# Load order of batch 0, opening tiles of the first product, and the place of one scale and two stores, in a linear-attention plus ELU-MLP kernel

## The chip, the cores and the metric

The kernel runs on one core of a Trainium2 chip. The metric is the device time of one execution in microseconds (us); the kernel before has a median of 288.38 us over 5 runs (287.56 to 288.8).

## The reference

```python
# attention, per batch b (8) and head h (8), 576 rows of 64
kv  = einsum('bhsd,bhse->bhde', k, v)
out = einsum('bhsd,bhde->bhse', q, kv)
x   = out / sqrt(mean(out*out, -1) + 1e-6) * g_norm      # then heads side by side: 4608 x 512
# MLP
h = x @ w_in                                             # 4608 x 2048
g = where(h > 0, h, exp(min(h, 0)) - 1)
y = g @ w_out                                            # 4608 x 512, float32
```

## The kernel before, in words

**Tiling.** The 4608 rows are worked in nine groups T = 0 to 8 of 512 rows. A group needs `xT[T]`, the normalised attention output turned so that the 512 features lie on partitions (four chunks of 128). The first product (`h_ps`, lines 382 and, at the start, 570) gives eight tiles i = 0 to 7 of 2 x 128 columns of `w_in`; each is an accumulation over the four chunks in a pair of PSUM banks, tagged A, B, or "mx" (one bank of the pool m, one of x). `elu` turns a tile into `gT` with an exponential on ScalarE (L350) and two VectorE instructions (L362, L366; the second reads PSUM and so sets when the pair is free again), or, where `relu` is given, with a Relu on ScalarE (L355) that frees the pair early. The second product (`o_ps`, L403) multiplies `gT` by `w_out`; ScalarE copies a result out (L419) and `store` sends halves of a group to memory through SyncE's queue (L461 to L464).

**The order is written by hand.** Each engine executes its instructions in the order in which the Python code emits them; a wait holds everything behind it on that engine or queue.

**The start (lines 468 to 652).** Batch 0 comes in chunks of heads: q chunks 0 and 2, k chunk 0 and v chunk 0 through SyncE's queue, the rest through GpSimd's load queue (`chunk_load`, L90; `load_w_in`, L116), which casts to bf16 on the way. Group 0 is normalised chunk by chunk: `chunk_kv` (L156), its copy `chunk_kv_out`, `chunk_y` (L189), `chunk_square` (L552), `mean_mm` (L199), an inverse root on ScalarE and `chunk_scale` (L212 on VectorE). `early(tiles, c)` issues the first product's matmuls (L570) of chunk c as soon as that chunk is there, in the order 0, 2, 1, 3, so that tiles are opened on chunk 0 and closed on chunk 3. `idle(n)` issues matmuls on zeros.

**The rest (lines 661 to 802).** In group T's window the attention part of group T+1 runs between the matmuls: `kv`, and for each half h of the rows `se` (product and squares), `sum` (L283), `inv` (L291, L292), `mul` (L299 on VectorE, then two DMA transposes on SyncE's queue, L306, which bring the scaled half into `xT`) and `gain` (L312 on VectorE, the multiplication by g_norm). `ahead` turns q of batch T+2 by two DMA transposes on SyncE's queue (L331); a copy on GpSimd (`gate`, L339) waits for them, and only then are the loads of the next batch issued. The dictionaries `early` and `late` say after which tile i each piece is emitted: `early` between tile i's matmuls and its `rest` (L362, L366), with the second-product half in `second[i]` emitted after the early pieces; `late` after the `rest`.

For T = 2 two tiles are *opened*: both get their matmuls over the first 256 rows (the half whose `gain0` comes first) before the second 256 rows are needed.

Of the kernel before, what the change touches and what calls it, by code (L numbers as in the profile page):

```python
# [16 lines left out]
def kernel(  # L17
# [16 lines left out]
    B, H, S, D = q.shape  # L34
# [5 lines left out]
    KC = DM // P  # L40
# [51 lines left out]
    def fetch_ahead(b):  # L92
        raw[b] = stage.tile([P, 4, RK, D], FP32, name="st_q", tag="q")
        load(raw[b], "q", b)
        for name in "kv":
            fetch(name, b)

    def cast_q(b):

        bf["q", b] = qkvp.tile([P, 2, RK, 2, D], BF16, name="q_bf", tag="q")  # L100
        for js in (slice(0, 3), slice(3, 6), slice(6, 9)):
            for u in range(2):
                nc.gpsimd.tensor_copy(  # L103
                    out=bf["q", b][:, u, js],
                    in_=raw[b][:, u::2, js, :].rearrange("p l j d -> p j l d"),
                )

    def copy_on(eng, out_, in_):
        if eng is nc.scalar:
            nc.scalar.copy(out_, in_)  # L110
        else:
            eng.tensor_copy(out=out_, in_=in_)  # L112

    def load_w_in(fs, cs=slice(0, KC)):
        cols = slice(fs.start * P, fs.stop * P)
        nc.gpsimd.dma_start(  # L116
            out=w_in_sb[:, cs, cols], in_=moe_w_in.rearrange("(c p) f -> p c f", p=P)[:, cs, cols]
        )
# [10 lines left out]
    def single(tag, name):  # L129
        pool = ps_x if tag == "x" else ps_m2  # L130
        return pool.tile([P, 512], FP32, name=name, tag=tag)

    def pair(tag, name):
        if tag in ("x", "m", "mx"):
            return [single(t, name) for t in (tag + tag)[:2]]
        return ps_m1.tile([P, 2, 512], FP32, name=name, tag=tag)
# [61 lines left out]
    def mean_mm(sq, ps):  # L198
        nc.tensor.matmul(ps, lhsT=ones, rhs=sq, start=True, stop=True)  # L199
# [4 lines left out]
    def r_tile():  # L204
        return outp.tile([P, 2, G], FP32, name="rT", tag="o")
# [5 lines left out]
    def scale_t(T, ps, r, cs, cols=slice(0, 512)):  # L211
        nc.vector.scalar_tensor_tensor(  # L212
            out=xT[T][:, cs, cols], in0=ps, scalar=g_col, in1=r, op0=ALU.mult, op1=ALU.mult
        )
# [113 lines left out]
    def turn_q(b):  # L328
        qt = qT_tile(b)
        for s in range(2):  # L330
            nc.sync.dma_start_transpose(  # L331
                out=qt[:, s].rearrange("p u j r -> p (u j) r"),
                in_=bf["q", b][s * 64 : s * 64 + 64].rearrange("p u j l d -> p (u j l d)"),
            )

    def after_turn(b):

        gate = const.tile([1, 2, 16], BF16, name="gate")
        nc.gpsimd.tensor_copy(out=gate, in_=qT[b][0:1, :, 1, RK - 1, 0:16])  # L339
# [35 lines left out]
    def g_tile(T):  # L375
        gT[T] = mlpg.tile([P, FC, G], BF16, name="gT", tag="gT")

    def mm1_part(T, i, ps, cs, cols=slice(0, 512), last=True):
        for a in range(2):
            f = 2 * i + a  # L380
            for n, c in enumerate(cs):
                nc.tensor.matmul(  # L382
                    (ps[a] if isinstance(ps, list) else ps[:, a, :])[:, cols],
                    lhsT=w_in_sb[:, c, f * P : f * P + P],
                    rhs=xT[T][:, c, cols],
                    start=(c == 0),
                    stop=(last and n == len(cs) - 1),
                )
# [62 lines left out]
    def mm2_half(T, i):  # L451
        mm2(T, i // 2, 8 * (i % 2), 8 * (i % 2) + 8)
# [31 lines left out]
    def chunk_load(name, cs):  # L484
        ms = slice(cs[0], cs[-1] + 1, 2)
        load(bf[name, 0][:, ms], name, 0, ms)
# [3 lines left out]
    chunk_load("q", (1, 3))  # L490
    chunk_load("k", (1,))
    chunk_load("v", (1,))
    load_w_in(slice(0, 6), slice(0, 1))
    chunk_load("k", (3,))
    chunk_load("v", (3,))
    for c in (2, 1, 3):
        load_w_in(slice(0, 6), slice(c, c + 1))
    for lo, hi in ((6, 8), (8, 12), (12, 16)):
        load_w_in(slice(lo, hi))
# [24 lines left out]
    def idle(n, ps):  # L524
        for _ in range(n):
            nc.tensor.matmul(ps, lhsT=zeros[:, 0:P], rhs=zeros, start=True, stop=True)
# [10 lines left out]
    def chunk_kv(kv_ps, c):  # L537
        kv_mm(0, [kv_ps[:, s, :] for s in range(2)], c % 2, (c // 2,))

    def chunk_kv_out(kv_ps, c, eng):  # L540
        rows, cols = slice(c // 2 * 64, c // 2 * 64 + 64), slice(c % 2 * 64, c % 2 * 64 + 64)
        copy_on(eng, kv_sb[rows, 0, c % 2], kv_ps[rows, :, cols])
# [3 lines left out]
    def chunk_y(c, ps):  # L546
        y_ps[c] = ps
        y_mm(0, c % 2, {c // 2: ps}, (c // 2,))

    def chunk_square(c):  # L550
        sq0[c] = attp.tile([P, G], BF16, name="sq", tag="sq")
        nc.scalar.activation(sq0[c], y_ps[c], AF.Square)  # L552

    def chunk_scale(c, r, cols=slice(0, 512)):
        scale_t(0, y_ps[c][:, cols], r[:, cols], c, cols)

    def chunk_norm(c, mean):

        r = r_tile()[:, 0, :]
        nc.scalar.activation(r, mean, AF.Ln, bias=eps_col)  # L560
        for n in range(2):
            cols = slice(n * 256, n * 256 + 256)
            nc.scalar.activation(r[:, cols], r[:, cols], AF.Exp, scale=-0.5)
            chunk_scale(c, r, cols)

    def early(tiles, c):

        for i, a in tiles:
            h = h_ps[i]
            nc.tensor.matmul(  # L570
                h[a] if isinstance(h, list) else h[:, a, :],
                lhsT=w_in_sb[:, c, (2 * i + a) * P : (2 * i + a) * P + P],
                rhs=xT[0][:, c, :],
                start=(c == 0),
                stop=(c == KC - 1),
            )
# [16 lines left out]
    mean = pair("A", "mean")[:, 0, :]  # L593
# [11 lines left out]
    r = r_tile()  # L605
    inv_t(r[:, 0, :], mean)
    mean = single("m", "mean")
# [5 lines left out]
    h_ps = [pair("A", "h_ps")]  # L613
# [4 lines left out]
    chunk_y(1, single("m", "y_ps"))  # L618
    chunk_square(1)
    chunk_scale(0, r[:, 0, :])  # L620
    chunk_scale(2, r[:, 1, :])
    early([(0, 0), (0, 1)], 0)
    mean = single("m", "mean")
    chunk_kv(kv_ps, 3)
    chunk_kv_out(kv_ps, 3, V)
    mean_mm(sq0[1], mean)
    r = r_tile()
    nc.scalar.activation(r[:, 0, :], mean, AF.Ln, bias=eps_col)
    y3 = single("x", "y_ps")
    h_ps += [None, [single("x", "h_ps"), None]]  # L630
    early([(2, 0)], 0)
    chunk_y(3, y3)
    chunk_square(3)
    for n in range(2):
        cols = slice(n * 256, n * 256 + 256)
        nc.scalar.activation(r[:, 0, cols], r[:, 0, cols], AF.Exp, scale=-0.5)
        chunk_scale(1, r[:, 0, :], cols)
    h_ps[1] = pair("B", "h_ps")
    early([(1, 0), (1, 1)], 0)
    early([(0, 0), (0, 1)], 2)  # L640
    mean_mm(sq0[3], mean)
    chunk_norm(3, mean)
    early([(2, 0), (1, 0), (1, 1)], 2)
    early([(0, 0), (0, 1), (1, 0), (1, 1), (2, 0)], 1)
    h_ps[2][1] = single("m", "h_ps")
    for c in (0, 2, 1):
        early([(2, 1)], c)
    early([(0, 0), (0, 1), (1, 0), (1, 1), (2, 0), (2, 1)], 3)
    for i in range(3):
        elu(0, i, h_ps[i], i == 1)()  # L650
    for i, tag in zip(range(3, 8), ("mx", "A", "B", "mx", "mx")):
# [116 lines left out]
    for T in range(2, NT):  # L768
        at, early, late = {}, {}, {}
        if T + 1 < NT:  # L770
            at = attention(T + 1)
            if T + 2 < B:
                cast_q(T + 2)

                def ahead(b=T + 2):
                    turn_q(b)
                    if b + 1 < B:
                        after_turn(b)
                        fetch_ahead(b + 1)
                at["ahead"] = ahead  # L780
            else:
                at["ahead"] = lambda: None
            early = {2: ("sum0", "inv0"), 4: ("sum1", "inv1"), 5: ("gain0",), 7: ("gain1",)}
            late = {0: ("kv",), 1: ("se0",), 2: ("mul0",), 3: ("se1",), 4: ("mul1", "ahead")}
        if T == 2:
            early = {2: ("sum0", "inv0"), 5: ("sum1", "inv1"), 6: ("gain0",), 7: ("gain1",)}
            late = {0: ("kv",), 1: ("se0",), 2: ("mul0",), 4: ("se1",), 5: ("mul1", "ahead")}
        halves = {1: 5, 3: 6, 5: 7} if T == 2 else {0: 1, 1: 3, 2: 4, 3: 5, 4: 6, 5: 7}
        second = {i: (lambda n=n: mm2_half(T - 1, n)) for i, n in halves.items()}
        if T > 2:  # L790
            window(T, at, early, late, second)
        else:
            g_tile(T)
            opened = [pair(tag, "h_ps") for tag in "BA"]
            for i in range(2):
                mm1_part(T, i, opened[i], range(KC), slice(0, 256))
            window(T, at, early, late, second, (3, 5), opened)
        mm2_half(T, 0)
        mm2_half(T, 2)
# [33 lines left out]
```

## Time and profile before

| quantity | value |
|---|---|
| median of 5 runs | 288.38 us (287.56 to 288.8) |
| the profiled execution's own time | 288.72 us |
| its span, first to last instruction | 286.2 us |
| TensorE matmul (PE) busy | 277.9 us, 97% |
| VectorE (DVE), ScalarE (ACT), GpSimd (POOL) busy | 57%, 49%, 17% |
| granted TensorE clock | 1.00 throughout |

Times in the views are microseconds from the span's start. PE and PEld are TensorE's matmuls and weight loads; SPq is SyncE's queue. A chain or timeline row gives start, duration, engine, line, output and input, and a count; brackets give the idle time before and what ended it. A row of the waits gives who waited for whom, the total, how often, and the longest. Ends of matmuls are modelled: one 128x512 matmul is shown as 0.38 us, but eight of them take 1.73 us in the chain, so one slot is 0.216 us.

### The profile page before, as it was taken

The numbers are of one execution on the slowest core, as the hardware profiler recorded it, in microseconds if no ns is written. First come the engines' busy times: TensorE is split into PE (matmuls) and PEld (weight loads), VectorE is DVE, ScalarE is ACT, GpSimd is POOL, SyncE is SP. The second block draws the span as 40 slices with busy tenths as digits, with TensorE's granted clock in tenths as the row PEclk, the third lists the DMA queues.
The fourth block names the chain that finished last, engine by engine and source line by source line (L and its number), as shares of the span: only waits on it lengthen the run. The fifth ranks groups of instructions, "written<-read, shape, count | busy, mean of one in ns | idle before, by whom it ended". The sixth has DMA issues, their size and how long they took to land.

```text
span 286.2 us, 5167 instructions
## 1 busy us (share of the span) xinstructions
PE 277.9 (97%) x2131; PEld 129.8 (45%) x2131; DVE 164.5 (57%) x222; ACT 141.4 (49%) x209; POOL 47.9 (17%) x89
## 2 busy tenths in 40 slices
PE   8899999999999899999999999999999999999994
PEld 3444444444644344444444444444444444444443
DVE  2439632966487547853776278727763776344600
ACT  4578359594468155425553455335543554333311
POOL 8643303203114033004200330000000000000000
PEclk9999999999999999999999999999999999999999
DMA  7999999999999769679936993632150235030222
GB/s 213 181 205 206 206 261 235 176 274 165 169 256 126 148 159 251 88 127 265 199 31 117 257 217 46 110 85 73 39 110 0 73 39 110 0 76 0 73 73 74
DMA packets 50571, 39.46 MB, mean 138 GB/s; under 512 B 30964, under 2 KB 44020, under 8 KB 50548
## 3 DMA queue, kind: packets, MB, share of 16 engines
q0 software_dynamic: 15008, 21.30, 37.2%
q1 hardware_dynamic: 35136, 17.31, 31.6%
q10 hardware_dynamic: 404, 0.53, 0.5%
q8 instruction: 16, 0.26, 0.4%
q14 instruction: 7, 0.06, 0.1%
HBM read 36.70 MB, written 9.44 MB: 161 GB/s over the span
## 4 chain that ended last, share of the span: by engine, by line
PE 87%; DMA 6%; DVE 3%; ACT 1%; issue 1%; POOL 0%; DVEq 0%; SPq 0%; POOLq 0%
PE o_ps L403 41%; PE h_ps L382 40%; DMA w_in_sb<-in_moe_w_in_dram 3%; DMA v_bf<-in_v_dram 2%; PE at L250 2%; PE at L156 1%; DVE gT L366 1%; PE o_ps L440 1%; DMA xT<-xs 1%; PE h_ps L570 1%; ACT elu_e L350 1%; DVE elu_e L362 1%; PE qt_ps L174 0%; DVE xs L299 0%; PE mean L199 0%
## 5 line engine op out<-in xcount | busy, mean ns | idle before, releaser
L382 PE MATMUL h_ps<-xT,w_in_sb 128*128 128x512 bf16 (+1 forms) x568 | 128.1, 373 | 2.1 <-DVE xT L312 1.2
L403 PE MATMUL o_ps<-w_out_sb,gT 128*128 128x512 bf16 x560 | 129.7, 379 | 0.0
L350 ACT ACTIVATE elu_e<-h_ps 128x1024 bf16<-128x1024 f32 (+1 forms) x79 | 74.0, 952 | 91.7 <-PE h_ps L382 89.8
L403 PEld LDWEIGHTS <-gT 128*128 128x128 bf16 x560 | 54.4, 98 | 65.6 <-issue 0.9
L382 PEld LDWEIGHTS <-w_in_sb 128*128 128x128 bf16 x568 | 53.9, 98 | 63.3 <-DVE xT L312 1.7
L366 DVE TENSOR_TENSOR gT<-elu_e,h_ps 128x1024 bf16<-128x1024 bf16 (+1 forms) x67 | 77.2, 1157 | 6.9 <-PE h_ps L382 0.5
L362 DVE TENSOR_SCALAR elu_e<-elu_e 128x1024 bf16<-128x1024 bf16 x72 | 31.5, 438 | 64.8 <-ACT elu_e L350 64.7
L419 ACT COPY o_sb<-o_ps 128x512 f32<-128x512 f32 x32 | 18.3, 587 | 21.1 <-PE o_ps L403 21.1
L103 POOL CAST q_bf<-st_q 128x384 bf16<-128x384 f32 x36 | 16.8, 510 | 36.7 <-DMA st_q<-in_q_dram 30.3
L283 DVE TENSOR_REDUCE ss<-sq 128x16 f32<-128x1024 bf16 x14 | 17.1, 1220 | 6.8 <-ACT sq L277 6.8
L299 DVE TENSOR_TENSOR xs<-at,ss 128x1024 bf16<-128x1024 f32 x14 | 17.0, 1218 | 1.2 <-ACT ss L292 1.2
L277 ACT ACTIVATE sq<-at 128x1024 bf16<-128x1024 f32 x14 | 14.4, 1028 | 0.0
L339 POOL COPY gate<-qT 1x32 bf16<-1x32 bf16 x5 | 1.0, 200 | 66.2 <-DMA qT<-q_bf 66.2
L212 DVE SCALAR_TENSOR_TENSOR xT<-y_ps,g_col,rT 128x512 bf16<-128x512 f32 (+1 forms) x10 | 6.1, 639 | 10.0 <-ACT rT L209 7.9
L312 DVE TENSOR_SCALAR xT<-xT,g_col 128x1024 bf16<-128x1024 bf16 x14 | 6.7, 480 | 5.1 <-DMA xT<-xs 5.0
L355 ACT ACTIVATE elu_h<-h_ps 128x1024 bf16<-128x1024 f32 (+1 forms) x12 | 9.3, 817 | 0.0
L156 PEld LDWEIGHTS <-k_bf 64*64 64x64 bf16 x576 | 6.3, 107 | 5.2 <-issue 4.7
L90 POOL DMA_DIRECT2D v_bf<-in_v_dram x11 | 7.6, 694 | 4.2 <-DMA w_in_sb<-in_moe_w_in_dram 2.1
L90 POOL DMA_DIRECT2D k_bf<-in_k_dram x11 | 7.7, 700 | 2.6 <-DMA w_in_sb<-in_moe_w_in_dram 1.8
L250 PEld LDWEIGHTS <-qT 64*128 64x128 bf16 (+1 forms) x248 | 4.3, 97 | 6.1 <-issue 5.9
L112 DVE COPY o_sb<-o_ps 128x256 f32<-128x256 f32 x1 | 0.4, 424 | 11.1 <-PE o_ps L440 11.1
L366 DVE TENSOR_TENSOR gT<-elu_e,elu_h 128x1024 bf16<-128x1024 bf16 x9 | 6.2, 692 | 0.9
(57 smaller groups left out, 102.2 us busy)
## 6 DMA issues: line engine op xcount, KB each, us to landing
st_q<-in_q_dram POOLq DMA_DIRECT2D x6, 1152.0 KB, 7.5
out_dram<-o_sb SPq DMA_DIRECT2D x24, 256.0 KB, 4.1
k_bf<-in_k_dram POOLq DMA_DIRECT2D x6, 576.0 KB, 9.9
v_bf<-in_v_dram POOLq DMA_DIRECT2D x6, 576.0 KB, 12.7
out_dram<-o_sb SPq DMA_DIRECT2D x19, 128.0 KB, 2.4
w_out_sb<-in_moe_w_out_dram POOLq DMA_DIRECT2D x4, 512.0 KB, 14.9
w_in_sb<-in_moe_w_in_dram POOLq DMA_DIRECT2D x2, 512.0 KB, 11.0
q_bf<-in_q_dram POOLq DMA_DIRECT2D x3, 288.0 KB, 13.4
```

The source lines that it names most:

```text
L90: eng.dma_start(out=dst.rearrange("p m j d -> p m (j d)"), in_=in_[:, ms, :])
L103: nc.gpsimd.tensor_copy(out=bf["q", b][:, u, js], in_=raw[b][:, u::2, js, :].rearrange("p l j d -> p j l d"),)
L250: nc.tensor.matmul(se_ps[lo:hi, l, (4 * i + m) * 64 : (4 * i + m) * 64 + 64], lhsT=qT[b][l * 64 : l * 64 + 64, s, u, j : j + n, :], rhs=kv ...
L277: nc.scalar.activation(sq, st["se", h], AF.Square)
L283: nc.vector.reduce_sum(out=ss, in_=st.pop(("sq", h)).rearrange("p l (m e) -> p (l m) e", e=D), axis=AX.X,)
L299: nc.vector.tensor_tensor(out=st["xs"][:, 2 * h : 2 * h + 2, :].rearrange("p i (l m e) -> p l i m e", l=2, e=D), in0=se_ps.rearrange("p l ...
L350: nc.scalar.activation(e[:, lo:hi, :], h, AF.Exp)
L362: nc.vector.tensor_scalar(out=e, in0=e, scalar1=1.0, scalar2=1.0, op0=ALU.min, op1=ALU.subtract)
L366: nc.vector.tensor_tensor(out=gT[T][:, 2 * i + lo : 2 * i + hi, :], in0=e[:, lo:hi, :], in1=h, op=ALU.add if relu else ALU.max,)
L382: nc.tensor.matmul((ps[a] if isinstance(ps, list) else ps[:, a, :])[:, cols], lhsT=w_in_sb[:, c, f * P : f * P + P], rhs=xT[T][:, c, cols] ...
L403: nc.tensor.matmul(o_ps[T, j], lhsT=gT[T][:, f, j * P : j * P + P], rhs=w_out_sb[:, f, :], start=(f == 0), stop=(f == FC - 1),)
L419: nc.scalar.copy(o_sb[T, half][:, j % 2, :], o_ps[T, j])
```

## The change

Three parts.

1. On the load queue, the first chunk of `w_in` is loaded after k and v chunk 3 instead of before them.
2. In the start, `early` on chunk 0 no longer stands ahead of `chunk_kv(3)` and `chunk_y(3)`: one idle matmul stands there, all five tile halves (0,0), (0,1), (1,0), (1,1), (2,0) are opened together behind `chunk_y(3)`, `chunk_scale(2)` moves behind `chunk_kv_out(3)` on VectorE, and the last matmuls are put so that tile 0 closes one matmul earlier.
3. In T = 2's window, `mul1` (the second scale of group 3, with its two transposes) moves from behind tile 5's `rest` and second-product half to ahead of both; and only tile 0 (pair B) is opened on half its rows, tile 1 gets whole 512-row matmuls at its turn.

```diff
-    load_w_in(slice(0, 6), slice(0, 1))
     chunk_load("k", (3,))
     chunk_load("v", (3,))
-    for c in (2, 1, 3):
+    for c in (0, 2, 1, 3):
         load_w_in(slice(0, 6), slice(c, c + 1))
...
     chunk_scale(0, r[:, 0, :])
-    chunk_scale(2, r[:, 1, :])
-    early([(0, 0), (0, 1)], 0)
-    mean = single("m", "mean")
+    idle(1, h_ps[0][:, 0, :])
     chunk_kv(kv_ps, 3)
     chunk_kv_out(kv_ps, 3, V)
+    chunk_scale(2, r[:, 1, :])
+    mean = single("m", "mean")
     mean_mm(sq0[1], mean)
...
-    early([(2, 0)], 0)
     chunk_y(3, y3)
     chunk_square(3)
+    h_ps[1] = pair("B", "h_ps")
+    early([(0, 0), (0, 1), (1, 0), (1, 1), (2, 0)], 0)
     for n in range(2):
...
-    h_ps[1] = pair("B", "h_ps")
-    early([(1, 0), (1, 1)], 0)
     early([(0, 0), (0, 1)], 2)
     mean_mm(sq0[3], mean)
     chunk_norm(3, mean)
-    early([(2, 0), (1, 0), (1, 1)], 2)
+    early([(1, 0), (1, 1), (2, 0)], 2)
     early([(0, 0), (0, 1), (1, 0), (1, 1), (2, 0)], 1)
     h_ps[2][1] = single("m", "h_ps")
-    for c in (0, 2, 1):
-        early([(2, 1)], c)
-    early([(0, 0), (0, 1), (1, 0), (1, 1), (2, 0), (2, 1)], 3)
+    early([(2, 1)], 0)
+    early([(2, 1)], 2)
+    early([(0, 0), (0, 1)], 3)
+    early([(2, 1)], 1)
+    early([(1, 0), (1, 1), (2, 0), (2, 1)], 3)
...
         if T == 2:
-            early = {2: ("sum0", "inv0"), 5: ("sum1", "inv1"), 6: ("gain0",), 7: ("gain1",)}
-            late = {0: ("kv",), 1: ("se0",), 2: ("mul0",), 4: ("se1",), 5: ("mul1", "ahead")}
+            early = {2: ("sum0", "inv0"), 5: ("sum1", "inv1", "mul1"), 6: ("gain0",), 7: ("gain1",)}
+            late = {0: ("kv",), 1: ("se0",), 2: ("mul0",), 4: ("se1",), 5: ("ahead",)}
...
-            opened = [pair(tag, "h_ps") for tag in "BA"]
-            for i in range(2):
-                mm1_part(T, i, opened[i], range(KC), slice(0, 256))
+            opened = [pair("B", "h_ps")]
+            mm1_part(T, 0, opened[0], range(KC), slice(0, 256))
             window(T, at, early, late, second, (3, 5), opened)
```

## The prediction

> **What bounds the kernel now.** I read the page first: PE is busy for 277.9 of 286.2 us, so a change pays only where PE stands still. Then the chain of waits in order of time, to see where it leaves PE:
>
> ```profile
> 7.72 9.24 DMA w_in_sb<-in_moe_w_in_dram
> ...
> 17.00 2.35 PE h_ps L570 x10
> ...
> 22.23 7.07 PE h_ps L382 x32
> ...
> 63.00 8.75 PE o_ps L403 x40
> ...
> 72.39 2.78 PE h_ps L382 x24
> ...
> 91.38 1.22 DVE xs L299
> ...
> 94.98 2.50 DMA xT<-xs
> ...
> 97.51 0.50 DVE xT L312
> ...
> 98.05 1.90 PE h_ps L382 x8
> ```
>
> After 98.05 it is PE without a break until 282.38. The waits of PE after the first ten us:
>
> ```profile
> PE h_ps L382 <- DVE xT L312: 1.2, 1, 1.2
> PE h_ps L382 <- ACT o_sb L419: 0.7, 1, 0.7
> ...
> PE h_ps L382 <- DVE gT L366: 0.3, 1, 0.3
> ```
>
> These are three places: the opening of T=3 (98.05), of T=2 (72.39) and tile 4 of T=0 (22.23). Two timelines say what is behind the first two: VectorE's between 61 and 76 us, and SyncE's queue between 60 and 104 us:
>
> ```profile
> 71.80 0.48 DVE L312 TENSOR_SCALAR xT<-xT,g_col 128x1024 bf16<-128x1024 bf16 x1 [1.88 <-DMA xT<-xs]
> 72.73 0.49 DVE L312 TENSOR_SCALAR xT<-xT,g_col 128x1024 bf16<-128x1024 bf16 x1 [0.44 <-DMA xT<-xs]
> ```
>
> ```profile
> 62.13 8.06 SPq L306 DMA_TRANSPOSE xT<-xs  x4
> ...
> 91.42 1.29 SPq L461 DMA_DIRECT2D out_dram<-o_sb  x2
> 92.80 3.44 SPq L306 DMA_TRANSPOSE xT<-xs  x2
> 96.33 3.59 SPq L331 DMA_TRANSPOSE qT<-q_bf  x2
> ```
>
> T=2 opens on a landing: VectorE is idle until the first half of xT is there, gain0 ends at 72.28 and PE starts at 72.39. The 0.7 is booked on the copy L419 only because that ends last (72.35); the first opened tile does not use its pair. T=3 opens on the second half of xT, whose transposes stand behind two stores.
>
> **Part 3, mul1 ahead of the stores.** sum1 (L283) ends at 90.33; ScalarE's two steps end at 90.70 + 0.22 = 90.92. The scale L299 starts at 91.38 only because tile 5's L362 and L366 (90.25, 90.77) stand ahead of it. Moved ahead of them it runs from 90.96 to 92.18. The transposes no longer follow the two stores: first issue at 92.24 instead of 92.80, taking about 1.25 us (the pair at 84.93 takes 2.60) instead of 2.13, so the second goes at 93.5 instead of 94.98. With its own 2.50 us to land: 96.0, gain1 to 96.5, PE at 96.55. PE is through with the work before at 93.26 + 16 x 0.216 = 96.72, so the stall in slots, 98.05 - 96.72 = 1.33 us, goes entirely, with 0.17 to spare. Bounds for the landing after the second issue: the shortest L306 row, 2.4 us, and the 3.8 us of the one issued at 92.80 beside the stores; the latter would leave PE at 97.85 and save 0.2. I take 2.5, the nearest row: batch 4's last load (issued 79.04, 12.7 us) is in at 91.7, and the stores now come after.
>
> What is late instead: L362 and L366 of tile 5 run at 92.1 to 93.3 (1.9 us later), but ScalarE's Relu (89.20 to 90.22) has freed that pair, and its gT is first read after T=3 opens. gain0 ends at 93.7, tile 6's L366, which frees pair B for T=3, at 95.4 instead of 94.82; PE wants B at 96.72. The stores are issued at 94.8 and 95.4, 3.4 us later; they now wait for the scale behind which they stand. Behind them stand batch 4's q transposes (L331), issued at 96.1 as before (96.33) but with 512 KB of stores just ahead. The window 92.5 to 95.0 shows the stores moving at 199 GB/s, 2.5 us; the q transposes began moving at 97.5 (0 GB/s from 97.0 to 97.5) and now begin at about 98.5: landing 103.7 instead of 102.7 (97.70 + 5.0), so d = 1.0 (bounds 0 and the whole 2.5). On them waits gate (102.85), on gate the loads of batch 5 (the last in at 104.87 + 12.4 = 117.3), and beside those loads land T=4's first transposes (issued 112.16, 5.6 us, 117.8), wanted by gain0 at 119.37 on VectorE. PE being 1.3 ahead, the want moves to 118.05. By d = 1.0 the landing is 118.8 at most; those transposes are issued 1.3 earlier, so some of it is regained, and I take 118.6. gain0 is then 0.55 late and with it L366 of tile 5, whose pair A tile 7 wants: before, it ends at 121.77 and tile 7 starts at 120.49 + 8 x 0.216 = 122.22, slack 0.45. Cost 0.1; ends 0 and, from 117.8 + 2.5 - 118.05 - 0.45, 1.8.
>
> The Trainium skill ("DMA: Bandwidth & Descriptors", Queues, rings and completion order) says that the descriptors of one ring start in order and that an engine takes turns between rings. That speaks against this part: the stores do not vanish from SyncE's ring, they only change whom they hold up. By that rule alone d would be the full 2.5, the cost below 1.8 and the sum 0.5 slower. The rows differ: part of the stores' time falls into a gap in the ring.
>
> **Part 3, one opened tile.** 32 half-matmuls at 0.109 (24 of them and the step to the next work take 72.39 to 75.10) become 16 of these and 8 of 0.216: saving below 0.05. Without the second opened tile the first half gives PE 8 x 0.109 = 0.87 us of work, to 73.26; the second half of tile 0 needs gain1, which ends at 73.22, PE 0.08 later as at 72.28/72.36. Loss 0.04; the price beyond is one to one with a later landing. Tile 1 now runs after kv at its turn; its pair A, copied out by 72.85, is free. Net 0, bounds -0.05 and, for a lag of 2 us between the halves, +1.0.
>
> **Parts 1 and 2, the start.** Loads: 144 KB of k or v take 0.7 us on the queue, and the last of batch 0 lands at 13.63. k3 and v3 come about 1.5 us earlier, w_in chunk 0 at 13.6 instead of 12.0; later loads keep their place, since the bytes ahead are the same. PE: chunk_kv(3) starts at 13.0 instead of 13.65 (one idle slot in place of two matmuls that waited 0.25), its copy ends at 13.8, chunk_y(3) runs at 13.97 instead of 14.59. But three matmuls that were done before are now behind it: 14.30 + 11 x 0.216 = 16.68 reaches chunk 1; before, 16.01 + 3 x 0.216 = 16.66. Both then wait for w_in chunk 1, landed 9.2 us after 7.72, at 16.92. After that, tile 0 closes one slot earlier, so tile 4 starts at 22.01 instead of 22.23. VectorE keeps up: scale(2) ends at 14.5, wanted at 15.2 by (2,0).
>
> The rows put chunk 1's landing at 16.92, chunk 2's at 14.55: 2.4 us for 192 KB, against 0.8 to the next. An instruction fetch of 16 KB falls between them (queue q8, 14.9). Earlier in PE's program it could hit chunk 2 instead: from a gain of 0.4 to a loss of 0.3 here.
>
> None of it reaches the end. What T=2 opens on hangs on loads, not on PE: GpSimd waits 11.4 us for batch 2's q (45.60), SyncE's queue 46.2 us for that cast (48.39), gate 6.6 us for the turned q (54.98), then batch 3's loads run to 71.1 (57.01 + 14.1), and the transposes issued at 62.13 take 9.0 us beside them against 2.5 later. PE is through at 62.93 + 40 x 0.216 = 71.57 and stands until 72.39. An earlier PE waits longer; a start later by up to 0.8 costs nothing. Term: 0, ends -0.4 and +0.1.
>
> **Sum.** -1.33 + 0.1 + 0 + 0 = -1.2 against the profiled execution: 288.72 (span 286.2 and 2.5 around it) becomes 287.5, span 285.0. That execution lay 0.34 above the median, so for the median 288.38 - 1.2 = 287.2. A change under 0.3% (0.87 us) can't be told from none here.
>
> **Rivals.**
>
> *The start's gain passes too* (10%). If the landings at T=2 move with PE after all, 0.2 to 0.4 more: 286.7. Against: the chain above, in which nothing waits for PE.
>
> *Half is given back* (24%): xT lands 3.2 to 3.8 us after its issue, or T=2's second half lags, or tile 7 of T=3 waits: 0.4 to 1.0 of the gain goes, 287.9. For it: over all 28 of L306 the median from issue to landing is 3.7 us.
>
> *Slower by the stores* (13%). The stores hold batch 4's q transposes, and so the loads beside T=4's first half. Place: L366 of tile 5 and tile 7's matmuls in T=3. Price: d - 0.7; at the bound 2.5, 1.8 us, so 288.9. It decides from d = 2.0, where it has eaten the 1.3. Against: the ring stood empty for half a microsecond before those q transposes, and nothing else reads them soon.
>
> *The change does nothing* (3%): were the 1.33 set by pair B or by VectorE and not by the landing. Against: VectorE is idle 2.7 us ahead of gain1 and B is free at 94.8. It would give 288.3.
>
> **How the numbers follow.** The forecast has 50%, its own range 286.8 to 287.6. With the first rival, down to 286.5; with most of the given-back case and the near end of the slower one, up to 288.7. Faster than 287.51: 46 of the forecast's 50, the first rival and a little of the second, 0.58. Within 0.3%: the rest of these, no change, and half of the slower one, 0.34. Slower than 289.25: that rival's far end with the 0.4 by which single runs lie off the median, 0.08.
>
> **What would show it.** Right: in SyncE's queue two L306 ahead of two L461 near 92 to 95; no wait of PE on L312 at the opening of T=3; the wait at T=2 grown to about 0.9. Wrong: PE's start of T=2 earlier by as much as tile 4 of T=0 (first rival), a wait of PE on L366 near tile 7 of T=3 or gate past 104.5 (third), gain1 still the last before T=3 (second).

## The result, and the profile after

The kernel after takes 287.05 us in the median (35 runs, 285.88 to 288.23), the kernel before, run beside it, 288.01 us (59 runs, 287.13 to 289.61). The ratio is 0.9963 with a 95% interval of 0.9954 to 0.9972: 0.96 us faster. The profiled execution has a span of 285.5 us (before 286.2) and a time of its own of 287.27 us. What lies around the span is 1.8 us here and was 2.5 us in the profiled execution of before. Over the runs it is 1.73 to 1.84 us in all 35 executions of after, but 1.9 to 2.9 us in 35 of the 71 of before whose spans were read. So spans compare better than single times: the median span over the runs of after is 285.3 us, against 286.0 to 286.2 for before, 0.7 to 0.9 us less; the rest of the 0.96 lies outside the span.

The waits of PE after the start are no longer the same ones. Columns: who waited for whom, total, how often, longest.

```profile
PE h_ps L382 <- DVE gT L366: 1.0, 1, 1.0
PE h_ps L382 <- DVE xT L312: 0.5, 1, 0.5
```

The second of them is T=2's opening. The first is new: in before the longest wait on L366 was 0.3 us. The timeline of PE in the kernel after places both, and shows T=3's opening without a wait:

```profile
71.51 1.92 PE L382 MATMUL h_ps<-xT,w_in_sb 128*128 128x256 bf16 x16 [0.53 <-DVE xT L312]
...
92.36 3.62 PE L403 MATMUL o_ps<-w_out_sb,gT 128*128 128x512 bf16 x16
95.82 1.89 PE L382 MATMUL h_ps<-xT,w_in_sb 128*128 128x512 bf16 x8
...
118.25 1.89 PE L382 MATMUL h_ps<-xT,w_in_sb 128*128 128x512 bf16 x8
121.18 1.89 PE L382 MATMUL h_ps<-xT,w_in_sb 128*128 128x512 bf16 x8 [1.04 <-DVE gT L366]
```

95.82 is T=3's opening: 92.36 + 16 x 0.216 = 95.82, so no slot is empty. 121.18 is tile 7 of T=3: the eight matmuls from 118.25 are through at 119.98, so 1.20 us are empty. SyncE's queue in the kernel after shows the moved scale's transposes ahead of the two stores, and the turning of q (L331) now directly behind these:

```profile
84.04 9.55 SPq L306 DMA_TRANSPOSE xT<-xs  x4
93.68 1.29 SPq L461 DMA_DIRECT2D out_dram<-o_sb  x2
95.06 4.33 SPq L331 DMA_TRANSPOSE qT<-q_bf  x2
```

The timeline of VectorE says what tile 7 waits for. gain0 of T=4 stands first and VectorE is idle ahead of it until the landing; the L366 that frees tile 7's pair comes only behind it:

```profile
115.99 1.22 DVE L299 TENSOR_TENSOR xs<-at,ss 128x1024 bf16<-128x1024 f32 x1
118.98 0.49 DVE L312 TENSOR_SCALAR xT<-xT,g_col 128x1024 bf16<-128x1024 bf16 x1 [1.77 <-DMA xT<-xs]
119.38 0.42 DVE L362 TENSOR_SCALAR elu_e<-elu_e 128x1024 bf16<-128x1024 bf16 x1
119.90 1.22 DVE L366 TENSOR_TENSOR gT<-elu_e,h_ps 128x1024 bf16<-128x1024 bf16 x1
```

The chain of waits names that landing as a piece of its own, `xT` from 111.19, 7.77 us long. It is the second of that half's two transposes, landing at 118.95, behind the last load of batch 5 (118.27). The copy that lets batch 5's loads go, in the kernel before and then in the kernel after:

```profile
102.85 0.20 POOL L339 COPY gate<-qT 1x32 bf16<-1x32 bf16 x1 [13.71 <-DMA qT<-q_bf]
```

```profile
102.34 0.20 POOL L339 COPY gate<-qT 1x32 bf16<-1x32 bf16 x1 [14.77 <-DMA qT<-q_bf]
```

**The last piece of the difference is at the end.** The last copy on VectorE, behind PE's last matmul, in the kernel before and then in the kernel after:

```profile
282.45 0.42 DVE L112 COPY o_sb<-o_ps 128x256 f32<-128x256 f32 x1 [11.10 <-PE o_ps L440]
```

```profile
281.77 0.42 DVE L112 COPY o_sb<-o_ps 128x256 f32<-128x256 f32 x1 [11.45 <-DMA out_dram<-o_sb]
```

PE's last matmul starts at 282.09 in before and at 281.05 in after, so the copy starts 0.36 us behind it in the one and 0.72 us in the other. With that, the 0.7 us between the two spans can be put together:

| place | before | after | change of span |
|---|---|---|---|
| T=2 opens | 72.39 | 71.51 | -0.88 |
| wait at T=3's opening (in slots) | 1.33 | 0 | -1.33 |
| wait at tile 7 of T=3 (in slots) | 0 | 1.20 | +1.20 |
| last copy behind the last matmul | 0.36 | 0.72 | +0.36 |
| sum | | | -0.65 |

In this profile the moved scale takes a wait away and nearly all of it comes back 25 us later. What remains came from T=2's opening, where the prediction had put nothing. The 0.88 us can be traced further. `chunk_y(1)`, which stands ahead of everything that the change moves, starts 0.35 us earlier in this execution (12.11, 12.46 in before). And the gate copy ahead of batch 3's loads runs 0.71 us earlier, in the kernel before and then in the kernel after:

```profile
54.98 0.20 POOL L339 COPY gate<-qT 1x32 bf16<-1x32 bf16 x1 [6.62 <-DMA qT<-q_bf]
```

```profile
54.27 0.20 POOL L339 COPY gate<-qT 1x32 bf16<-1x32 bf16 x1 [6.41 <-DMA qT<-q_bf]
```

The last of these loads took 14.1 us from issue to landing in both. That is one execution of each kernel, and the landing on which T=2 opens differs from run to run; so the experiments had to say what each part is worth.

### The profile page after: what moved, and what is told of

It is laid out like the page before. It is cut to its first block, busy times and chain, and to the rows that moved or that the text cites. A ratio compares the mean times of both kernels' runs of the same rounds, so it can differ in the third digit from the quotient of the medians.

```text
span 285.5 us, 5152 instructions
## 1 busy us (share of the span) xinstructions
PE 277.2 (97%) x2124; PEld 129.1 (45%) x2124; DVE 164.9 (58%) x222; ACT 141.3 (50%) x209; POOL 49.2 (17%) x89
## 4 chain that ended last, share of the span: by engine, by line
PE 85%; DMA 8%; DVE 3%; ACT 1%; issue 0%; SPq 0%; DVEq 0%
PE h_ps L382 38%; PE o_ps L403 38%; DMA xT<-xs 6%; DMA first_v<-in_v_dram 2%; PE h_ps L569 2%; PE at L156 1%; PE at L250 1%; DVE gT L366 1%; PE kv_ps L156 1%; ACT elu_e L350 1%; PE y_ps L189 1%; PE qt_ps L174 1%; PE mean L199 1%; PE o_ps L440 1%; DMA out_dram<-o_sb 1%; DVE ss L283 0%
## 5 line engine op out<-in xcount | busy, mean ns | idle before, releaser
L382 PEld LDWEIGHTS <-w_in_sb 128*128 128x128 bf16 x560 | 53.1, 98 | 63.3 <-issue 1.7
L366 DVE TENSOR_TENSOR gT<-elu_e,h_ps 128x1024 bf16<-128x1024 bf16 (+1 forms) x67 | 77.2, 1157 | 6.6
L419 ACT COPY o_sb<-o_ps 128x512 f32<-128x512 f32 x32 | 18.3, 587 | 21.1 <-PE o_ps L403 21.1
L103 POOL CAST q_bf<-st_q 128x384 bf16<-128x384 f32 x36 | 17.8, 537 | 34.5 <-DMA st_q<-in_q_dram 34.5
L312 DVE TENSOR_SCALAR xT<-xT,g_col 128x1024 bf16<-128x1024 bf16 x14 | 6.7, 481 | 4.7 <-DMA xT<-xs 4.7
L366 DVE TENSOR_TENSOR gT<-elu_e,elu_h 128x1024 bf16<-128x1024 bf16 x9 | 6.3, 704 | 0.8
```

What stands on the lines that cost most here:

```text
L103: nc.gpsimd.tensor_copy(out=bf["q", b][:, u, js], in_=raw[b][:, u::2, js, :].rearrange("p l j d -> p j l d"),)
L366: nc.vector.tensor_tensor(out=gT[T][:, 2 * i + lo : 2 * i + hi, :], in0=e[:, lo:hi, :], in1=h, op=ALU.add if relu else ALU.max,)
L382: nc.tensor.matmul((ps[a] if isinstance(ps, list) else ps[:, a, :])[:, cols], lhsT=w_in_sb[:, c, f * P : f * P + P], rhs=xT[T][:, c, cols] ...
L419: nc.scalar.copy(o_sb[T, half][:, j % 2, :], o_ps[T, j])
```

## The experiments

The theory after the result (A): moving the scale alone gives little, because the stores now stand ahead of batch 4's q and the delay is paid at tile 7 of T=3; the start and the single opened tile are worth something whenever T=2's landing is early. The rival (B) is the prediction as written: the scale nets 1.2 us, the start nothing, the single opened tile nothing. Four experiments ran on each of three chips; those of one chip share the runs of before there (288.38, 288.05 and 287.83 us).

### The scale alone

```diff
-            early = {2: ("sum0", "inv0"), 5: ("sum1", "inv1"), 6: ("gain0",), 7: ("gain1",)}
-            late = {0: ("kv",), 1: ("se0",), 2: ("mul0",), 4: ("se1",), 5: ("mul1", "ahead")}
+            early = {2: ("sum0", "inv0"), 5: ("sum1", "inv1", "mul1"), 6: ("gain0",), 7: ("gain1",)}
+            late = {0: ("kv",), 1: ("se0",), 2: ("mul0",), 4: ("se1",), 5: ("ahead",)}
```

The base is the kernel before.

> The kernel before with one edit: the second scale of group 3 and its two transposes ahead of tile 5's rest and of the stores. Theory A (the gain at the opening of T=3 is given back three tiles later): the wait of PE on L312 at the opening of T=3 (1.33 us in slots) is gone, the transposes L306 stand ahead of the two stores L461, but tile 7 of T=3 waits for L366 of tile 5 by 0.8 to 1.3 us, because gain0 of T=3 waits for its landing; total faster by 0 to 0.5 us, ratio 0.998 to 1.000. Theory B (the prediction: the give-back is 0.1): faster by 1.2 us, ratio 0.996.

Measured: 287.58 us (286.99 to 289.17, 12 runs) beside 288.38; ratio 0.9988 (0.9973 to 1.0003). By the ratio that is 0.35 us, with 0 inside the interval and the predicted 1.2 us outside; by the medians it is 0.8 us, by the medians of the spans 0.6 (285.6, 286.2). The waits of PE in this kernel:

```profile
PE h_ps L382 <- DVE gT L366: 0.9, 2, 0.6
PE h_ps L382 <- ACT o_sb L419: 0.6, 1, 0.6
```

There is no wait on L312 any more, so T=3 opens without one. The row on L419 is T=2's opening at 72.24. Of the two waits on L366 one is tile 4 of T=0, as in before; the other, 0.6 us (0.80 in slots), is at tile 7, the one that after has. So the give-back belongs to the scale's move and needs neither the new start nor the single opened tile.

### The start alone

Parts 1 and 2 of the change on the kernel before (the diff's first four pieces); T=2's and T=3's windows are as before.

> The kernel before with the load order and the new start alone (parts 1 and 2), T=2's window as before. Theory A (the start's gain reaches the end, because the opening of T=2 moves with the load queue): T=2 opens 0.5 to 0.9 us earlier than at 72.39, the waits at T=3's opening and elsewhere stay, total faster by 0.6 to 0.9 us, ratio 0.997 to 0.998. Theory B (the prediction: what T=2 opens on does not move): ratio 1.000, and the wait at T=2's opening is longer by what the start saves.

Measured: 287.77 us (287.05 to 289.77, 12 runs); ratio 0.999 (0.9969 to 1.001). PE waits on L312 twice, 1.9 us together: T=3's opening as before, and at T=2's opening, where PE is now through at 71.28 and starts at 72.32. In this profile the start is absorbed, as predicted; the interval does not tell 0 from 0.6 us, which is what the medians alone would give.

### Tile 7's wait taken away from VectorE's side

```diff
+        if T == 3:
+            early = {2: ("sum0", "inv0"), 4: ("sum1", "inv1"), 6: ("gain0",), 7: ("gain1",)}
```

The base is the kernel after; gain0 of T=4 moves behind tile 5's L366, so that a late landing no longer holds that L366.

> The changed kernel with one more edit: in T=3's window gain0 is emitted with tile 6 instead of tile 5, so that tile 5's L366 no longer stands behind it on VectorE. Theory A: the wait of PE on L366 at tile 7 of T=3 (1.2 us in slots) is gone and no other takes its place; against the changed kernel 1.0 to 1.2 us faster, ratio to the kernel before 0.992 to 0.993. Theory B (tile 7 waits for something else, or the wait only moves on to T=4's opening): ratio 0.996 as the changed kernel.

Measured: 286.44 us (285.81 to 289.85, 9 runs); ratio 0.9942 (0.9923 to 0.9961). The wait on L366 at tile 7 is gone from its profile. The kernel after stands at 0.9963; the difference is 0.6 us in the median, but the two intervals overlap. The profiled execution of this kernel is its slowest, and shows what else is at play: PE waits at T=2's opening for the landing of xT, 2.2 us in that execution.

```profile
PE h_ps L382 <- DVE xT L312: 2.2, 1, 2.2
```

### Tile 7's wait taken away from the queue's side

```diff
-            early = {2: ("sum0", "inv0"), 5: ("sum1", "inv1", "mul1"), 6: ("gain0",), 7: ("gain1",)}
-            late = {0: ("kv",), 1: ("se0",), 2: ("mul0",), 4: ("se1",), 5: ("ahead",)}
+            early = {2: ("sum0", "inv0"), 5: ("sum1", "inv1", "mul1", "ahead"), 6: ("gain0",), 7: ("gain1",)}
+            late = {0: ("kv",), 1: ("se0",), 2: ("mul0",), 4: ("se1",)}
```

The base is the kernel after; batch 4's q is turned ahead of the two stores, too.

> The changed kernel with one more edit: the two transposes of batch 4's q (L331), the gate and the loads behind it are emitted ahead of tile 5's second-product half, so that on SyncE's queue they stand ahead of the two stores. Theory A (the stores in the ring hold up q, gate, the loads of batch 5, and by these T=4's first half): gate is passed about 1 us earlier than at 102.3, T=4's first half lands about 1 us earlier, and the wait at tile 7 of T=3 falls from 1.2 to 0.2 or less; ratio to the kernel before 0.992 to 0.994. Rival (the landing is late because PE, and with it the need, is earlier, and the loads run as long as before): gate moves, the wait at tile 7 stays above 0.7 us, ratio 0.995 to 0.996.

Measured: 286.25 us (285.78 to 286.86, 6 runs); ratio 0.9939 (0.9921 to 0.9956). SyncE's queue in this kernel, and then GpSimd's timeline:

```profile
93.67 3.59 SPq L331 DMA_TRANSPOSE qT<-q_bf  x2
97.35 1.97 SPq L461 DMA_DIRECT2D out_dram<-o_sb  x2
```

```profile
99.96 0.20 POOL L339 COPY gate<-qT 1x32 bf16<-1x32 bf16 x1 [12.40 <-DMA qT<-q_bf]
```

The gate copy runs at 99.96 instead of 102.34, all of batch 5's loads move with it, and tile 7 does not wait. The two runs take away the same wait by different means and arrive within 0.2 us of each other: what the kernel after loses at tile 7 comes out at 0.6 to 0.8 us in the median, not the predicted 0.1. Both intervals still touch that of the kernel after, because T=2's landing varies in all three kernels.

### What T=2's opening hangs on, and who can use it

Three idle matmuls in front of T=1's last results, on the kernel after:

```diff
         o_ps[1, j] = ps[:, j, :]
+    idle(3, o_ps[1, 0])
```

> The kernel after with three idle matmuls (3 x 0.216 = 0.65 us of TensorE) in front of the last work before T=2 opens. Theory A (T=2 opens on the landing of xT's first half, not on TensorE): TensorE stands 0.0 to 0.1 us there instead of the 0.7 of the kernel after wherever the landing is as there, T=2's opening and all behind it stay, and the time is that of the kernel after, 287.0 us or at most 0.2 more (ratio to before 0.996 to 0.997). Theory B (what the start gains passes through T=2's opening to the end, so TensorE's own time counts there): 0.65 us more than the kernel after, 287.7 us (ratio 0.999). Between them, 0.3 us more, if the landing comes early in about half of the executions.

Measured: 287.21 us (286.57 to 289.41, 12 runs); ratio 0.9973 (0.9947 to 0.9999). That is 0.16 us more than the kernel after by the medians and 0.3 by the ratios, and the two were not run side by side. In its profile the landing came late of its own accord (gain0 at 72.01 instead of 70.92), so PE still waited 0.76 us there. The time lies between the theories and does not decide.

The single opened tile alone, on the kernel before:

```diff
-            opened = [pair(tag, "h_ps") for tag in "BA"]
-            for i in range(2):
-                mm1_part(T, i, opened[i], range(KC), slice(0, 256))
+            opened = [pair("B", "h_ps")]
+            mm1_part(T, 0, opened[0], range(KC), slice(0, 256))
```

> The kernel before with only one tile of T=2 opened on half its rows, nothing else. Theory A (the prediction's term): nothing, 288.0 us, the two gains 0.9 us apart and the first half's work of 0.87 us covers the lag. Theory B (a lag between the halves is no longer covered by a second opened tile): TensorE waits a second time at T=2's opening, on the second half's multiplication, 0.3 to 1.0 us, ratio 1.001 to 1.003.

Measured: 288.04 us (286.93 to 288.59, 12 runs) beside 288.05; ratio 0.9991 (0.9968 to 1.0015). On its own it does nothing to the median that these runs can tell, and the spans show no gain either (median 286.3, before 286.0). What it does change lies around the span. In these 12 executions that time is at most 1.83 us, while 14 of the 30 of before on the same chip have 1.97 to 2.93. It is so in all runs: with two opened tiles (before and four of the experiments) 58 of 117 executions have 1.9 us or more, with one opened tile 1 of 100 (2.07); the means are 2.08 and 1.79 us. So the single opened tile takes about 0.3 us from the mean outside the span. A 16 KB read on the instruction queue q8 starts 1.0 to 1.8 us behind the last instruction in four of the five profiles with two opened tiles and in none of the nine with one. Where it starts 1.6 us or more behind, the time around the span is 2.3 to 2.6 us, in the other two of the five it is 1.8. That this read makes the time longer was not tested.

The scale and q ahead of the stores on the kernel before, with the old start and two opened tiles (the edit to the two dictionaries as above):

> The kernel before with group 3's second scale ahead of the stores and batch 4's turning of q ahead of them too; the start and the two opened tiles are as before. Theory A (the start's 0.35 to 0.7 us is absorbed at T=2's opening): as fast as the kernel after with q ahead of the stores, 286.3 us (ratio to before 0.994), and no wait of TensorE at T=3's opening or at tile 7 of T=3. Theory B (the start passes): 0.4 to 0.7 us slower than that one, 286.8 us (ratio 0.9965).

Measured: 287.21 us (286.3 to 288.6, 12 runs); ratio 0.9973 (0.9948 to 0.9998). Compared with the kernel that has the new start and one opened tile as well, 0.96 us slower (0.0034 by the ratios; the two were on different chips, and the intervals just overlap). So parts 1 and 2 and the single opened tile come out at nearly a microsecond together once the rest does not wait, though neither showed anything alone. By the spans it is 0.8 us (285.25, 284.45); the rest lies around them. The timeline of PE at T=2's opening shows one half of it:

```profile
71.45 1.04 PE L382 MATMUL h_ps<-xT,w_in_sb 128*128 128x256 bf16 x8
72.77 1.91 PE L382 MATMUL h_ps<-xT,w_in_sb 128*128 128x256 bf16 x16 [0.29 <-ACT o_sb L419]
```

Here xT's landing is early (gain0 at 70.81) and the first opened tile starts without a wait. Its eight half-matmuls end at 71.45 + 8 x 0.109 = 72.32; the second opened tile takes the pair from which ScalarE copies T=1's last results, 71.65 to 72.72 in this profile, and starts at 72.77, 0.45 us late. With one opened tile nothing asks for that pair so early.

Batch 3's k loaded ahead of the gate, on the kernel with q ahead of the stores:

```diff
-            bf[name, b] = qkvp.tile([P, 4, RK, D], BF16, name=f"{name}_bf", tag=name)
+            bf[name, b] = qkvp.tile([P, 4, RK, D], BF16, name=f"{name}_bf", tag=name, bufs=4 if name == "k" else 3)
...
         for name in "kv":
-            fetch(name, b)
+            if (name, b) not in bf:
+                fetch(name, b)
...
     fetch_ahead(2)
+    fetch("k", 3)
     cast_q(2)
```

(The other allocation of these buffers gets the same count. Line numbers of this kernel and of those built on it are one higher.)

> The kernel after with q's transposes ahead of the stores, and batch 3's k loaded before the gate instead of behind it (a fourth buffer of k). Theory A (T=2's opening hangs on the landing of xT beside batch 3's loads): with one load of three less behind the gate, v of batch 3 is in about 4 us earlier, xT's first half lands at once, TensorE's wait at T=2's opening of 0.7 us goes, and the start's gain now passes: 0.5 to 0.8 us below the 286.25 us of the kernel with q ahead of the stores, 285.6 us (ratio to before 0.9915). Theory B (the landing is late for another reason, such as the transposes' own place in the queue): the wait at T=2 stays at 0.7 us and the time at 286.25 us. A third outcome: k of batch 3 now delays batch 2's k and v or their casts, and a wait turns up before T=2.

Measured: 285.74 us (285.60 to 285.98, 7 runs); ratio 0.9916 (0.9884 to 0.9947). It beats both kernels, the kernel before by 2.3 us. The timeline of VectorE at T=2's opening:

```profile
69.44 0.48 DVE L313 TENSOR_SCALAR xT<-xT,g_col 128x1024 bf16<-128x1024 bf16 x1
71.00 0.49 DVE L313 TENSOR_SCALAR xT<-xT,g_col 128x1024 bf16<-128x1024 bf16 x1 [1.07 <-DMA xT<-xs]
```

gain0 runs without an idle time in front of it, PE goes through T=2's opening at 71.06, and no wait on L313 or L367 is left in its list. The landing of that load came 2.8 us earlier than in after (batch 3's v issued at 57.46 and landed 10.2 us later, against 56.30 and 14.1), where I had written 4. What tells most is the spread: 0.4 us over 7 runs, against 2.4 us over the 35 of after and 1.1 us over 6 with q ahead of the stores alone (standard deviations 0.15, 0.61 and 0.39 us). That suggests that the run-to-run differences of the kernel after are for the most part T=2's landing.

### Each part taken away from the quiet kernel

On that base, called quiet because T=2's opening does not wait in it, one part at a time was put back as it was (in the last of the four, two). The four ran on one chip together, the base (285.74 us) on another, so differences to the base carry what the chips differ by; `chunk_y(1)`, which stands ahead of everything that differs, starts at 12.22 in the base's profile and at 12.49 to 12.69 in these four. In the four profiles of the base's chip it starts at 12.11 to 12.32, so 0.2 to 0.5 us of each difference below may be the chip, or the execution, and not the part.

The old start and load order:

```diff
+    load_w_in(slice(0, 6), slice(0, 1))
...
-    for c in (0, 2, 1, 3):
+    for c in (2, 1, 3):
...
-    idle(1, h_ps[0][:, 0, :])
...
+    early([(0, 0), (0, 1)], 0)
...
+    early([(2, 0)], 0)
...
-    early([(0, 0), (0, 1), (1, 0), (1, 1), (2, 0)], 0)
...
+    early([(1, 0), (1, 1)], 0)
...
```

> The kernel with k of batch 3 ahead (285.74 us, T=2's opening no longer waits for a landing), with the start and load order of before put back, nothing else. From the first normalised product to tile 4 of T=0 the kernels with the old start took 9.77 to 9.95 us, this kernel's start 9.38. Theory A (the start is worth its 0.4 to 0.6 us as soon as T=2's opening does not wait): 286.2 us. Theory B (it is absorbed at some other place): 285.75 us.

Measured: 286.23 us (286.13 to 286.53, 6 runs), 0.49 us more. Inside the profile the part can be read without that doubt. Tile 4 of T=0 starts at 22.30, 9.81 us behind `chunk_y(1)` at 12.49; in the base it is 9.38 us. The 0.43 us are still there at the end: from tile 4 to the last matmul both take 257.8 us. The wait that the change removes at tile 4 is back in the timeline of PE:

```profile
22.30 7.07 PE L383 MATMUL h_ps<-xT,w_in_sb 128*128 128x512 bf16 x31 [0.31 <-DVE gT L367]
```

Two opened tiles again (the diff of the single opened tile, turned round):

> The kernel with k of batch 3 ahead, with two tiles of T=2 opened again. Theory A (the second opened tile takes the pair that T=1's last results leave only when ScalarE has copied them out, so with xT early TensorE waits for that copy): a wait of 0.3 to 0.5 us on the copy at L420 of this kernel, 286.1 to 286.3 us. Theory B (one or two opened tiles are worth the same, the prediction's net 0): 285.75 us.

Measured: 286.57 us (286.43 to 287.24, 10 runs), 0.83 us more. PE in its timeline waits for the copy, as it did with the scale and q ahead on the old start:

```profile
71.34 1.04 PE L383 MATMUL h_ps<-xT,w_in_sb 128*128 128x256 bf16 x8
72.67 1.91 PE L383 MATMUL h_ps<-xT,w_in_sb 128*128 128x256 bf16 x16 [0.29 <-ACT o_sb L420]
```

In slots 72.67 - 71.34 - 0.87 = 0.46 us; the remainder to 0.83 is the later start of that profile (`chunk_y(1)` at 12.63, 0.41 behind the base's). Theory A's wait is there and its size fits; the time overshot its 0.5 by what lies ahead of the change.

q behind the stores again, the scale still ahead of them:

> The kernel with k of batch 3 ahead, but with batch 4's turning of q behind the stores, as in the kernel after. Theory A (the stores ahead of the turned q delay batch 5's loads, and with them T=4's first half and tile 7 of T=3): gate 2 to 2.5 us later, near 102, gain0 of T=4 waits for its landing until about 118.5, a wait of 0.8 to 1.6 us at tile 7 of T=3, 286.6 to 287.2 us. Theory B (the prediction's 0.1 us): 285.85 us.

Measured: 286.37 us (286.09 to 286.73, 6 runs), 0.63 us more. The gate copy runs at 102.21 (base 99.47), and the timeline of VectorE shows gain0 of T=4 waiting:

```profile
117.85 0.49 DVE L313 TENSOR_SCALAR xT<-xT,g_col 128x1024 bf16<-128x1024 bf16 x1 [0.81 <-DMA xT<-xs]
```

At tile 7 PE lost 0.25 us in that execution (its two tiles from 118.07 take 3.71 instead of 3.45 us), less than the 0.8 to 1.6 I had expected: the landing was a microsecond earlier than in after. Another 0.29 us of the 0.63 is the later start of this profile (`chunk_y(1)` at 12.51). So the give-back at tile 7 is 0.25 to 1.2 us from one execution to another; the medians put it at 0.6 to 0.8 in the kernel after, and here at 0.63 with what the chips differ by in it. This kernel is also the kernel after with the k load moved and nothing else: that alone makes it 0.68 us faster by the medians (287.05, 286.37) and 0.5 by the ratios (0.9963, 0.9946), with 0.64 us between its 6 runs.

The scale and q both behind the stores, as in before:

> The kernel with k of batch 3 ahead, but with the second scale of group 3 and the turning of q both where before has them, behind tile 5's rest. T=3's opening waits 1.1 to 1.5 us on the second half of xT, as before. Theory A (most of what moving the scale alone gains is given back at tile 7): this is 0.2 to 0.6 us slower than the run with only q behind the stores, 287.1 to 287.5 us. Theory B (moving the scale alone nets the predicted 1.2 us): 1.2 us slower than that run.

Measured: 286.36 us (286.19 to 286.91, 7 runs): the same as with the scale alone ahead, where theory A expected 0.2 to 0.6 us more and theory B 1.2. The timeline of PE has T=3's wait back:

```profile
96.97 1.90 PE L383 MATMUL h_ps<-xT,w_in_sb 128*128 128x512 bf16 x8 [1.08 <-DVE xT L313]
```

So on a kernel that waits nowhere else, moving the scale alone gains nothing that can be told: the two ran on one chip, and their ranges, 286.09 to 286.73 and 286.19 to 286.91, lie over each other; 1.2 us can be excluded, a few tenths cannot. Moving it together with q is worth 0.62 us by the medians, with what the chips differ by in it. This profile is the slowest of its seven runs. In slots the wait is 1.24 us in it (92.27 + 16 x 0.216 = 95.73, then 96.97), and not all of that is gained by the move, for the last copy says that some is lost again: with the scale in its new place it starts 0.72 us behind the last matmul in all ten profiles, with the scale in its old place 0.36 us in all four. 1.24 - 0.36 = 0.88 would be left of this execution's wait; why the medians show less is not settled.

## Why the prediction was right, point by point

The time (287.2 forecast, 287.05 measured) and the side were right, in part by luck. The change was 0.96 us and not 1.2, and started from a base that came out at 288.01 over 59 runs instead of 288.38; by the spans it was only 0.7 to 0.9. The working was right in one step and wrong in several that happened to balance.

- **The scale's own effect: right.** T=3's opening lost its 1.33 us entirely, with the scale on VectorE from 89.84 (the idle time ahead of it ends on the inverse root, as worked out) and the second half landing 2.5 us after its issue, the price taken.
- **"Cost 0.1; ends 0 and ... 1.8": mis-sized.** The mechanism stood in the text as it happened: stores ahead of q, gate, batch 5's loads, T=4's first half, gain0, L366, tile 7. The delay d was not the error: the turning of q was issued 1.27 us earlier than in before (95.06, 96.33) and the gate copy ran 0.51 us earlier (102.34, 102.85), so d, counted from the issue, was 0.76; the text's 1.0 is 1.2 when counted so (103.7 - 96.1 against 102.7 - 96.33). What failed was the slack. gain0 came at 118.98, 0.4 later than the 118.6 taken: the text started from 117.8, the landing of the first of the half's two transposes, while gain0 waits for both, and the second had landed at 118.26 in before. And it was wanted earlier than the 118.05 taken, because T=2 itself had opened 0.88 us earlier and the want moves with PE while the landing does not. It cost 1.20 us in the profile and 0.6 to 0.8 in the medians. By the rule of the Trainium skill as the prediction read it ("DMA: Bandwidth & Descriptors", Queues, rings and completion order) d would have been 2.5, which the gate copy does not show; that rule's direction, against this part, was right all the same. The "some of it is regained" showed nowhere: T=4's first half, issued 2.2 us earlier than in before, took 7.8 us to land instead of 4.9, and landed just behind the last of batch 5's loads (118.27).
- **"None of it reaches the end": wrong as a rule.** The start was held to be absorbed at T=2's opening. It is, in an execution where xT lands late (1.0 us of wait with the start alone). In the profile of after the wait did not grow to the 0.9 us foreseen; T=2's opening moved forward by 0.88 us, the first of the two signs the text had named for being wrong that were met. The other was the wait on L366 at tile 7. The text held that nothing in the chain of these loads waits for the start. But the gate copy runs at 54.27 to 54.68 in the five profiles with the new start and at 54.73 to 55.16 in the four with the old one (the kernels with k ahead left out). What blurs it is the landing: batch 3's v then took 12.7 to 15.9 us, and landed at 69.5 to 72.6 in the five and at 70.1 to 71.1 in the four. Where it does not hold PE up, as with k ahead, the start's 0.43 us passes through. One profiled execution had been read as if its wait were a property of the kernel. The start's own gain was also larger than the 0.22 us worked out: chunk 1 of `w_in`, taken at 16.92 again, landed at 14.98, and the slow step fell ahead of chunk 3 (17.06). The text's "0.8 to the next" was 0.4 in before (16.96, 17.37).
- **One opened tile, "Net 0, bounds -0.05": wrong in the bound.** The text saw that the copy L419 ends last and dismissed it, since in that execution the first tile covered it. With an early landing the second opened tile waits 0.45 us for the pair that this copy empties. The bound on the gain side should have been -0.45. The time around the span, shorter by 0.3 us in the mean with one opened tile, was not a term at all.
- **A term that was missing.** The last copy costs 0.36 us more with the scale in its new place.

Of the rivals, "the start's gain passes too" (10%) and "half is given back" (24%) both came true in part, in opposite directions. The sum by the runs: scale alone -0.35 (by the ratio, 0 to 0.8), start alone -0.3, single opened tile alone -0.26, each with an interval that holds 0; together -0.9, and the change measured -0.96. The near addition of these three is arithmetic on uncertain numbers, and the third of them is not in the spans (their means are 0.04 us longer than before's there). What the runs show is that the scale's move gives back most of what it gains, and does not carry the 0.96 alone.

What stays open: why batch 3's loads take a different time in each execution, and why the last copy is later. For the latter the trace shows that VectorE executes 319 instructions ahead of that copy in the ten profiles with the scale in its new place, and 320 in the four with the old. A gap of 0.40 to 0.42 us stands between the two last waits in front of the copy in these four, and directly in front of the copy in the ten. In all 14 profiles an 8 KB read on the instruction queue q14 starts 0.65 to 0.92 us behind the end of that gap, wherever the gap stands. That fits a step in fetching VectorE's instructions, which the last copy meets or not by its place in the count; no run tested it.

## What to carry to other kernels

Here a wait that ended on a DMA landing was a draw, not a constant: before a gain ahead of it is costed at nothing, look at how far the landing moves between executions and what the transfer's own issue waits for, and cost the term with both ends. When a transfer is moved ahead of stores, move the transfers that gate later loads along with it, or the stores' time is only handed on: here the scale alone was worth little or nothing that could be told, and turning q ahead of the stores as well about 0.6 to 0.8 us more by the medians, with the chips' difference in it. And taking one load of three out from behind a gate took the wait at T=2 and most of the run-to-run spread away: as the only edit to the kernel after it gave 0.5 to 0.7 us, and its 6 runs lie within 0.6 us, against 2.4 for the 35 of after.

## What was not expected of the hardware

- The same 576 KB load, issued at the same place in the program behind the same two others, landed 12.7 to 15.9 us after its issue in nine profiles. The product that waits for the transposes issued beside it started 0.5 to 0.8 us behind that landing each time, and PE's wait at that place ran from 0 to 2.2 us.
- Two transposes of q issued 3.7 us ahead of 512 KB of stores instead of behind them brought the copy that waits for them 2.4 us forward (102.34 to 99.96); 1.4 us of that is their own earlier issue (95.06 to 93.67).
- Moving one VectorE instruction and two transposes in the middle of the kernel moved the last copy, some 190 us later, by 0.36 us against PE, in the same direction in every profile.
- The time around the span depends on the kernel: with one opened tile 1.73 to 1.85 us in 99 of 100 executions, with two 1.9 to 2.9 in half of 117.
